# One values' scale per pair of heads, q and k casts on ScalarE, and a planner that prices float32r weight loads

## The chip, the cores and the metric

One core of a Trainium2 chip runs the whole kernel. The metric is device time in microseconds (us) of one execution; lower is better. The engines are named as the profile names them: PE (TensorE matmuls), PEld (its weight loads), DVE (VectorE), ACT (ScalarE), POOL (GpSimd) and SP (SyncE, which issues every DMA of this kernel).

## What is computed

```python
# q, k, v: (2, 8, 768, 64); centroids: (8, 16, 64)
q_assign = argmax(einsum('bhsd,hcd->bhsc', unit(q), unit(centroids)), -1)
k_assign = argmax(einsum('bhsd,hcd->bhsc', unit(k), unit(centroids)), -1)
scores = where(q_assign[..., :, None] == k_assign[..., None, :], q @ k.T / 8, -1e9)
attn = softmax(scores)
x = heads_side_by_side(attn @ v)                 # (1536, 512)
h = x @ w_in;  x = (h - tanh(h)) @ w_out         # d_ff 2048
out = (sigmoid(x @ w_gate) * (x @ w_val)) @ w_out2   # d_ff 1536
```

## The kernel before

The 16 heads (2 batches of 8) go through attention in 8 pairs; then two feed-forward blocks run over 1536 tokens. Each float32 operand is split into a high float32r part and a low rest, and a product is three matmuls, or one with the parts stacked on the partitions. Exponentials and values are split in the same way into two float16 parts; for that the values are first multiplied by a power of two, the *scale* `sv`.

A head passes these steps. `pair_prep(s)`: SP loads `rawq` and `rawk` of the pair, PE transposes them (line 504), ACT copies them out into `xtq`, `xtk` (L508), PE makes the cluster scores (L532), DVE finds the largest in five operations (L544 to L554), PE transposes the one-hot rows (L566), ACT writes them to `oht` (L572). The high parts of q and k, `hlq` and `hlk`, are cast by DVE (L513), the low parts by POOL (L520). SP then copies q, k and one-hot rows into a stack of each head (`stk`, three buffers; L245). `head_max(h)`: six tiles of 128 queries; PE computes each tile's high-part scores into one of three PSUM buffers (`ba`, `bb`, `bc`; L638), DVE takes each row's maximum (L642); PE and DVE turn the maxima into one row (`mt`), and SP puts it into the stack. `head_attend(h)`: six tiles again; PE makes the full scores (L673, L674), ACT takes each tile's exponential twice, in float32 (`pf`) and in float16 (`pt` or `ptt`; L677), POOL or DVE subtracts the two (L687), and PE multiplies with the values (L704 to L706, 108 matmuls a head), after which DVE divides (L719 to L721).

The scale: `v_scale(b)` makes one number for each batch. Four loads by `v_part` bring the whole batch's values into `pt` buffers, which are not otherwise used yet; DVE takes the largest magnitude of each (L441) and of the four (L458), PE transposes the result (L459), DVE makes a power of two and its reciprocal in four one-partition operations (L453 to L456), PE spreads it to all partitions (L461), DVE writes `sv` (L463). Each pair's values are loaded a second time into the one buffer `rawv` (L612), scaled by ACT to the high part (L616) and by DVE to the low part (L619).

Nothing of this order is written by hand. Every step is a `Task` with an engine, a cost, a priority, the tasks it needs and the buffers it takes. `Planner.run` walks through time as it models it and gives each engine, again and again, the ready task with the least priority number among those that can start within `AH_<engine>` of the first one. The instructions are issued in that order, and each engine, SP's queue too, keeps it on the chip. The table `PRM` holds the numbers from which priorities are made (`ZH` for the casts, `ZOT` for the one-hot rows, and so on). While PE has nothing to do at the start, it runs `N_BUSY` = 140 fillers of two matmuls (L423).

In the planner of before a PE task costs a fixed time, doubled while the planner thinks that the clock is low:

```python
cost = t.cost if self.warm else 2 * t.cost
```

Of the kernel before, what the change touches and what calls it, by code (L numbers as in the profile page):

```python
# [18 lines left out]
P = 128  # L19
# [7 lines left out]
PRM = dict(  # L27
    QUEUE=2.4775, AH_PE=0.086, AH_ACT=0.2978, AH_DVE=0.0374, AH_POOL=1.0538, AH_SP=0.8944, N_BUSY=140, NR=2,
    NRH=1, HX=['hx', 'hhxx'], WAR=0.797, LM=9, LV=8, ZP1=-12.75, ZP=1.801, FD=0.173, FO=0.6467, LOQ=0, VHI=0,
    VL=2.416, VLS=1.907, VR=17.393, ZSV=-28.212, ZRAW=19.311, ZT=0.914, ZH=36.739, ZHL=14.119, ZS=4.321,  # L30
    ZC=-8.823, ZOT=-37.186, ZD=22.995, ZDH=0.679, ZDM=3.94, ZVL=25.343, ZVS=33.74, ZX=-1.228, ZE=36.766,
    ZLOW=18.842, ZLOWP=2.75, SEMS=1.0, TC=0.2839, TW=0.9257, M2=1, ZQK=0.25, ZMS=-24.119, Z0=52.817, HB=92.235,
    NB4=5, ROWS=0.0155, VB=7.706, RAWL=2.2, NMID=2, NPL2=2, W1L=0.695, D1L=0.565, W2L=1.385, D2L=-1.014,
    ZI=7.332, ZJ=-3.277, PORT=0.12)


class Task:
# [3 lines left out]
    __slots__ = ("eng", "cost", "lat", "fn", "deps", "prio", "take", "end", "n", "duty", "port")  # L41

    def __init__(self, eng, cost, prio, fn, deps=(), take=(), lat=0.0, duty=1.0, port=None):
        self.eng, self.cost, self.prio, self.fn = eng, cost, prio, fn
        self.port = eng == "POOL" if port is None else port
        self.deps, self.take, self.lat, self.duty = [d for d in deps if d is not None], list(take), lat, duty
        self.end = None
# [9 lines left out]
class Planner:  # L57
# [10 lines left out]
    def __init__(self):  # L68
        self.tasks, self.kinds, self.clock = [], {}, {}
        self.count, self.coming, self.retire = {}, {}, {}  # L70
        self.first = {}
        self.link, self.port = 0.0, 0.0
        self.busy, self.window, self.warm = {}, 0, False

    WINDOW = 3.413

    def tensor_time(self, start, t):
# [5 lines left out]
        cost = t.cost if self.warm else 2 * t.cost  # L83
        a, end = start, start + cost
        while a < end:
            w = int(a / self.WINDOW + 1e-9)
            e = min(end, (w + 1) * self.WINDOW)
            self.busy[w] = self.busy.get(w, 0.0) + (e - a) * t.duty
            a = max(e, a + 1e-6)
# [34 lines left out]
    def run(self):  # L124
# [16 lines left out]
        while todo:  # L141
            best = None
            for eng, lst in ready.items():
                now = self.clock.get(eng, 0.0)
                can = []
                for at, t in lst:
                    start = max(now, at)
                    if t.lat:
                        start = max(start, self.link - self.QUEUE)
                    for kind in {s.kind for s in t.take}:  # L150
                        n = sum(s.kind == kind for s in t.take)
                        free = sorted(f[0] + self.lag(f[1], eng) for f in self.kinds.get(kind, ()))
                        if len(free) < n:
                            break
                        start = max(start, free[n - 1])
                    else:
                        can.append((start, t.prio, t.n, t))
                if can:
                    first = min(c[0] for c in can)
                    c = min((c for c in can if c[0] <= first + self.AHEAD[eng]), key=lambda c: c[1:3])  # L160
# [49 lines left out]
def tile_cluster_attention_moe(  # L210
# [164 lines left out]
    sv = const.tile([P, B], F32, name="sv")  # L375
    vm = const.tile([P, B, HP + 1], F32, name="vm")
    e = const.tile([1, B, 2], F32, name="e")
# [33 lines left out]
    t_c3 = add(PE, 0.11, -30, lambda: nc.tensor.transpose(at(z_sm)[0:D, 0:H * C], cn, ident), [t_c2], [z_sm])  # L411
# [13 lines left out]
    fill = [add(PE, 0.107, 1e6, keep_busy) for i in range(N_BUSY)]  # L425
# [5 lines left out]
    t_sv = []  # L431

    def v_part(b, i, z):
        buf = Slot("pt")

        def flat_buf():
            return at(buf).bitcast(F32).rearrange("p a n -> p (a n)")
# [6 lines left out]
    def v_scale(b):  # L444
        z = PRM["VL"] + b * PRM["VB"]
        parts = [v_part(b, i, z + i * PRM["VLS"]) for i in range(HP)]
        z += HP * PRM["VLS"] + PRM["ZSV"]
        sc = Slot("sm")
        i32 = mybir.dt.int32
        x, y, top = e[:, b, 0:1], e[:, b, 1:2], vm[:, b, HP:]  # L450

        def v_top():
# [27 lines left out]
    def pair_prep(s):  # L480
# [8 lines left out]
        for x, (nm, src) in enumerate((("q", q), ("k", k))):  # L489
# [8 lines left out]
            ev[nm], tts = [], []  # L498
            for half in range(2):
# [10 lines left out]
                tt = use(raw, add(PE, 0.33, z + PRM["ZT"] + PRM["ZQK"] * x + half, tr, [ld] + tts, [sm] + ([xt] if half == 0 else [])))  # L510
                tts.append(tt)
                ev[nm].append(use(sm, add(ACT, c_act(HALF), z + PRM["ZT"] + PRM["ZQK"] * x + half, evac, [tt] + ev[nm])))
            hi_t[nm] = add(DVE, c_dve2(S), z + PRM["ZH"] + PRM["ZQK"] * x, lambda xt=xt, hls=hls: nc.vector.tensor_copy(  # L513
                at(hls)[:, 0], at(xt)), ev[nm], [hls], port=True)
            lo_t[nm] = []
            for half in range(2):
# [4 lines left out]
                                                            op=ALU.subtract), [hi_t[nm]]))  # L521
            use(xt, hi_t[nm], *lo_t[nm])
# [12 lines left out]
        s0 = add(PE, 0.86, z + PRM["ZS"] + 0.0, lambda: score(0), ev["q"] + ev["k"] + [t_cb], [sm], duty=0.75)  # L535
        s1 = add(PE, 0.86, z + PRM["ZS"] + 0.1, lambda: score(1), [s0], duty=0.75)
        s2 = add(PE, 0.86, z + PRM["ZS"] + 0.2, lambda: score(2), [s1], duty=0.75)
# [3 lines left out]
        def scores():  # L541
            return at(sm)[:, 0:G * C].rearrange("p (g c) -> p g c", c=C)

        m0 = add(DVE, c_dve(G * C), z + PRM["ZC"] + 0, lambda: nc.vector.tensor_reduce(  # L544
            at(mm)[:, 0, :, 0], scores(), axis=AX.X, op=ALU.max), [s2], [mm])
        m1 = add(DVE, c_dve(G * C), z + PRM["ZC"] + 0, lambda: nc.vector.tensor_tensor(
            scores(), scores(), at(mm)[:, 0].to_broadcast([P, G, C]), op=ALU.is_equal), [m0])
        m2 = add(DVE, c_dve(G * C), z + PRM["ZC"] + 0, lambda: nc.vector.tensor_tensor(
# [941 lines left out]
```

## Time and profile before

| | us |
|---|---|
| median of 3 runs (795.37 to 795.73) | 795.71 |
| the profiled execution's own time | 795.33 |
| its span, first to last instruction | 793.5 |
| busy in the span: PE / PEld | 777.7 / 728.7 |
| busy in the span: DVE / ACT / POOL | 576.0 / 438.0 / 565.0 |

Of the execution's time 1.8 us lie outside the span. Attention fills roughly the first 260 us and the feed-forward blocks the rest. Matmuls overlap in PE's pipeline, so that "busy" on PE says that something is in flight, not that PE is at its peak; two things have to be read beside it, the distance from one matmul's start to the next, and how many of the matmuls are fillers. The granted clock is TensorE's, as a share of 2.4 GHz.

### The profile page before, as it was taken

What the parts mean: (1) busy time and instruction counts of PE and PEld (TensorE: products, weight loads), DVE (VectorE), ACT (ScalarE), POOL (GpSimd) and SP (SyncE); (2) the same over time, 40 slices, a digit from 0 to 9 for tenths busy, and PEclk for the clock granted to TensorE, in tenths of its full rate; (3) what the DMA queues carried; (4) which work ended last, traced back from release to release, by engine and by line L of the source; (5) the groups of instructions that cost most, each with busy time, mean ns of one, the idle gap of its engine ahead of it and who ended that gap; (6) DMA issues with size and microseconds to landing.
All of it is one profiled execution on the core that took longest, in us unless ns stands there. A gap on an engine that the chain in (4) does not pass through costs nothing.

```text
span 793.5 us, 15831 instructions
## 1 busy us (share of the span) xinstructions
PE 777.7 (98%) x5919; PEld 728.7 (92%) x5919; DVE 576.0 (73%) x1076; ACT 438.0 (55%) x852; POOL 565.0 (71%) x597
## 2 busy tenths in 40 slices
PE   9999999999999999999999999999999999999998
PEld 9777889888879999999999999999999989999996
DVE  4967987797987878967577678996456576666424
ACT  4267787878886645544454455655553535344240
POOL 4078777876898995888678688979584856748331
PEclk9989999999999999999999999999999999999999
DMA  9775666465543000422122132113211222221004
GB/s 220 201 173 139 155 156 138 110 152 141 150 135 102 29 1 0 134 67 80 57 78 67 42 113 86 40 56 106 67 40 67 81 80 81 67 66 41 1 1 159
DMA packets 69340, 72.93 MB, mean 92 GB/s; under 512 B 30256, under 2 KB 52880, under 8 KB 69264
## 3 DMA queue, kind: packets, MB, share of 16 engines
q1 hardware_dynamic: 69264, 71.93, 33.0%
q8 instruction: 46, 0.75, 0.4%
q14 instruction: 30, 0.25, 0.1%
HBM read 48.27 MB, written 3.15 MB: 65 GB/s over the span
## 4 chain that ended last, share of the span: by engine, by line
PE 84%; DVE 8%; issue 5%; ACT 2%; POOL 1%; DMA 0%; DVEq 0%; POOLq 0%; ACTq 0%
PE over_left L974 18%; PE over_left L1293 16%; PE over_right L974 13%; PE over_right L1293 9%; PE sm L974 6%; PE sm L1293 6%; DVE finr L642 2%; PE sm L704 2%; PE sm L705 2%; PE sm L706 1%; PE sm L532 1%; PE sm L504 1%; PE bb L673 1%; PE ba L673 1%; PE ba L638 1%
## 5 line engine op out<-in xcount | busy, mean ns | idle before, releaser
L687 POOL TENSOR_TENSOR pt<-pf,pt 128x768 f16<-128x768 f32 x45 | 75.5, 1691 | 28.1 <-ACT pt L677 13.1
L687 POOL TENSOR_TENSOR ptt<-pf,ptt 128x768 f16<-128x768 f32 x34 | 58.0, 1724 | 41.2 <-ACT ptt L677 34.1
L1000 ACT ACTIVATE stk<-pf 128x384 fp32r<-128x384 f32 x43 | 22.6, 524 | 37.7 <-POOL pf L1323 12.4
L1001 POOL TENSOR_TENSOR stk<-pf,hlq 128x384 fp32r<-128x384 f32 x22 | 22.7, 1030 | 27.8 <-ACT hlq L1000 27.8
L1293 PE MATMUL over_left<-xh,stk 128*128 128x384 f32 x138 | 41.5, 336 | 0.0
L974 PE MATMUL over_left<-stk,w 128*128 128x384 f32 x158 | 39.4, 335 | 0.0
L704 PE MATMUL sm<-vs,pt 128*128 128x65 f16 x324 | 38.2, 194 | 0.4 <-DVE xl L741 0.4
L642 DVE TENSOR_REDUCE finr<-ba 128x1 fp32r<-128x768 f32 x35 | 33.2, 947 | 7.1 <-PE ba L638 7.0
L705 PE MATMUL sm<-vs,pt 128*128 128x64 f16 x324 | 38.1, 195 | 0.0
L706 PE MATMUL sm<-vs,pt 128*128 128x65 f16 x324 | 37.7, 192 | 0.2 <-POOL pt L687 0.2
L1313 DVE TENSOR_TENSOR pf<-over_left,pf 128x384 f32<-128x384 f32 x42 | 23.3, 554 | 19.8 <-ACT pf L1309 12.3
L642 DVE TENSOR_REDUCE finr<-bc 128x1 fp32r<-128x768 f32 x32 | 30.3, 948 | 6.6 <-PE bc L638 6.4
L704 PEld LDWEIGHTS <-pt 128*128 128x128 f16 x324 | 29.9, 96 | 5.5 <-issue 5.4
L677 ACT ACTIVATE pf<-bb 128x768 f32<-128x768 f32 x34 | 27.9, 822 | 10.8 <-PE bb L674 7.4
L677 ACT ACTIVATE pf<-ba 128x768 f32<-128x768 f32 x31 | 25.5, 823 | 15.0 <-PE ba L674 13.2
L1001 POOL TENSOR_TENSOR stk<-pf,stk 128x384 fp32r<-128x384 f32 x25 | 26.6, 1063 | 7.7 <-ACT stk L1000 7.5
L705 PEld LDWEIGHTS <-pt 128*128 128x128 f16 x324 | 30.3, 97 | 0.7 <-issue 0.5
L706 PEld LDWEIGHTS <-pt 128*128 128x128 f16 x324 | 30.4, 99 | 0.3 <-POOL pt L687 0.3
L642 DVE TENSOR_REDUCE finr<-bb 128x1 fp32r<-128x768 f32 x29 | 27.5, 947 | 4.3 <-PE bb L638 4.2
L705 PE MATMUL sm<-vs,ptt 128*128 128x64 f16 x252 | 30.2, 195 | 0.3 <-DVE vs L619 0.3
L704 PE MATMUL sm<-vs,ptt 128*128 128x65 f16 x252 | 30.3, 193 | 0.0
L706 PE MATMUL sm<-vs,ptt 128*128 128x65 f16 x252 | 30.1, 192 | 0.0
(575 smaller groups left out, 3167.8 us busy)
## 6 DMA issues: line engine op xcount, KB each, us to landing
vs<-in_moe_w_out_dram SPq DMA_DIRECT2D x48, 256.0 KB, 2.6
stk<-hlq SPq DMA_DIRECT2D x32, 192.0 KB, 2.7
stk<-hlk SPq DMA_DIRECT2D x16, 384.0 KB, 4.2
vs<-in_moe_w_in_dram SPq DMA_DIRECT2D x24, 256.0 KB
vs<-in_moe_w_gate_dram SPq DMA_DIRECT2D x24, 256.0 KB
vs<-in_moe_w_val_dram SPq DMA_DIRECT2D x24, 256.0 KB, 2.7
rawq<-in_q_dram SPq DMA_DIRECT2D x16, 192.0 KB, 3.0
rawk<-in_k_dram SPq DMA_DIRECT2D x16, 192.0 KB, 4.6
```

The source lines that it names most:

```text
L642: rd.append(use(mx, add(DVE, c_dve(S), z + t, lambda t=t, mx=mx: nc.vector.tensor_reduce(at(mh)[:, t:t + 1], at(mx)[:, :, 0:HALF], axis=AX ...
L673: nc.tensor.matmul(o, at(sk)[0:K1, 1, ts], at(sk)[0:K1, 0, c], start=True, stop=False)
L677: nc.scalar.activation(o.rearrange("p (j n) -> p j n", j=2), at(st)[:, :, 0:HALF], AF.Exp, scale=scale)
L687: lambda nce=nc.vector if on_v else nc.gpsimd, pf=pf, pt=pt: nce.tensor_tensor(at(pt)[:, 1], at(pf), at(pt)[:, 0], op=ALU.subtract), [e0, ...
L704: nc.tensor.matmul(oview()[:, t], ph, vv[:, 0:D + 1], start=(kt == 0), stop=False)
L705: nc.tensor.matmul(oview()[:, t, 0:D], ph, vv[:, D + 1:2 * D + 1], start=False, stop=False)
L706: nc.tensor.matmul(oview()[:, t], plo, vv[:, 0:D + 1], start=False, stop=(kt == T - 1))
L974: nc.tensor.matmul(ps, a, b, start=(i == 0), stop=(i == n - 1))
L1000: a = add(ACT, c_acts(CH), z, lambda: nc.scalar.activation(hi(), src(), AF.Copy), deps, take)
L1001: b = add(POOL, c_pool(CH), z, lambda: nc.gpsimd.tensor_tensor(lo(), src(), hi(), op=ALU.subtract), [a])
L1293: nc.tensor.matmul(at(bank[to])[:, 0:CH], lh, rh, start=start and i == 0, stop=stop and i == 3 * KH - 1, skip_group_check=True)
L1313: return use(x, use(bank[n], add(DVE, c_dve(CH), rank[0], lambda: nc.vector.tensor_tensor(at(x), ps(n), at(x), op=ALU.add), deps)))
```

## The change

- **Scale.** `v_scale` is called from `pair_prep` and makes one scale for each pair of heads out of the pair's own `rawv`, which is there for the scaling anyway. The eight extra loads into `pt` and the reduction over four parts are gone; the chain of DVE reduction (now L447), PE transpose (L451), four DVE operations (L442 to L445), PE spread (L453) and `sv` (L455) runs 8 times where it ran twice. The scaling on ACT and DVE now waits for its own pair's chain.
- **Casts.** With `NHA` = 8 all 16 casts of q and k to the high part go from DVE (`nc.vector.tensor_copy`) to ACT (`nc.scalar.activation`, L503).
- **Planner.** A PE task carries the time `tail` of its last matmul. A task of float32r matmuls (no `tail` given) costs up to `LOAD` = 0.111 more when PE comes to it with no matmul before it that is long enough to load its weights behind. `duty` is gone.
- **Numbers.** `N_BUSY` is 155 and nearly all of `PRM` is new. `PVG` = 1 leaves the tasks of the value products as they were.

```diff
-    ZC=-8.823, ZOT=-37.186, ZD=22.995, ZDH=0.679, ZDM=3.94, ZVL=25.343, ZVS=33.74, ZX=-1.228, ZE=36.766,
+    ZOT=-40.532, ZD=21.696, ZDH=1.444, ZDM=3.94, ZVL=25.343, ZVS=16.581, ZX=-1.228, ZE=23.426, ZLOW=24.325,
...
         cost = t.cost if self.warm else 2 * t.cost
+        if t.tail is None:
+            cost += max(0.0, self.LOAD - (self.tail if start - self.clock.get("PE", 0.0) < 0.02 else 0.0))
+        self.tail = self.LOAD if t.tail is None else t.tail
...
-        ld = add(SP, DMA_C, z, lambda: dma(flat_buf().rearrange("p (h n) -> p h n", h=2), v[
-            b, 2 * i:2 * i + 2].rearrange("h (p t) d -> p h (t d)", t=T)), take=[buf], lat=1.2)
-        return use(buf, add(DVE, c_dve(2 * T * D), z + PRM["VR"], lambda: nc.vector.tensor_reduce(
-            vm[:, b, i:i + 1], flat_buf(), axis=AX.X, op=ALU.max, apply_absolute_value=True), [ld]))
...
-        t1 = add(DVE, 0.08, z, lambda: nc.vector.tensor_reduce(top, vm[:, b, 0:HP], axis=AX.X, op=ALU.max), parts)
-        t2 = add(PE, 0.11, z, lambda: nc.tensor.transpose(at(sc)[0:1, 0:P], top, ident), [t1], [sc])
+        t1 = add(DVE, c_dve(2 * T * D), z + PRM["VR"], lambda: nc.vector.tensor_reduce(
+            top, at(rv).rearrange("p h t d -> p (h t d)"), axis=AX.X, op=ALU.max, apply_absolute_value=True), [ld])
+        use(rv, t1)
+        z += PRM["ZSV"]
+        t2 = add(PE, 0.11, z, lambda: nc.tensor.transpose(at(sc)[0:1, 0:P], top, ident), [t1], [sc], tail=0.111)
...
-            hi_t[nm] = add(DVE, c_dve2(S), z + PRM["ZH"] + PRM["ZQK"] * x, lambda xt=xt, hls=hls: nc.vector.tensor_copy(
-                at(hls)[:, 0], at(xt)), ev[nm], [hls], port=True)
+            if s < PRM["NHA"]:
+                hi_t[nm] = [add(ACT, c_acts(S), z + PRM["ZH"] + PRM["ZQK"] * x, lambda xt=xt, hls=hls: nc.scalar.activation(
+                    at(hls)[:, 0], at(xt), AF.Copy), ev[nm], [hls])]
...
+        t_sv = v_scale(s, rv, lv, z + (PRM["ZV0"] if s == 0 else 0), smk)
...
-                    [lv, t_sv[b]] + [x[0] for x in vts], [vs] if hh == 0 else [])
+                    [t_sv] + [x[0] for x in vts], [vs] if hh == 0 else [])
```

Where the instructions stand now is shown at three places.

SP's queue around the first copy of a maxima row (`stk_0<-mt_0`, head 0). Before:

```order
L439 DMA pt_5_101<-in_v_dram 128x2x384
L245 DMA stk_0_86<-mt_0_115 1x6x128
L439 DMA pt_6_102<-in_v_dram 128x2x384
L439 DMA pt_7_103<-in_v_dram 128x2x384
L494 DMA rawq_0_120<-in_q_dram 128x6x64 x2
L494 DMA rawk_0_123<-in_k_dram 128x6x64 x2
L245 DMA stk_1_87<-mt_1_116 1x6x128
L245 DMA stk_2_88<-hlq_0_122 64x768
L612 DMA rawv_0_92<-in_v_dram 128x2x384
L245 DMA stk_0_86<-hlq_0_122 64x768
L245 DMA stk_2_88<-hlk_0_125 64x2x768
```

With the change:

```order
L483 DMA rawk_0_123<-in_k_dram 128x6x64 x2
L249 DMA stk_0_86<-mt_0_115 1x6x128
L249 DMA stk_2_88<-hlq_0_122 64x768
L606 DMA rawv_0_92<-in_v_dram 128x2x384
L249 DMA stk_2_88<-hlk_0_125 64x2x768
L249 DMA stk_2_88<-oht_0_128 16x768 x2
L249 DMA stk_2_88<-hlq_0_122 32x768
L249 DMA stk_2_88<-hlk_0_125 32x768
```

The loads of values into `pt` are gone from here, and the copies into `stk_2`, the stack of head 2, stand right behind the first `mt`; before they stood behind the second one and behind four loads.

ACT in the exponentials of head 1. Before (`pf` and `pt` are exponentials, `vs` values, `oht` one-hot rows):

```order
L677 ACTIVATE pf_0_107<-bc_0_618 128x768
L616 ACTIVATE vs_1_90<-rawv_0_92,sv_170 128x6x64
L677 ACTIVATE pf_2_109<-bb_0_80 128x768
L616 ACTIVATE vs_1_90<-rawv_0_92,sv_170 128x6x64
L677 ACTIVATE pf_1_108<-ba_0_76 128x768
L677 ACTIVATE pt_2_98<-ba_0_76 128x768
L677 ACTIVATE pf_0_107<-ba_0_76 128x768
L572 ACTIVATE oht_0_128<-sm_1_72,row_b_163,row_w_160 64x768
```

With the change (`hlk` is a cast):

```order
L672 ACTIVATE pf_2_109<-bc_0_637 128x768
L672 ACTIVATE ptt_8_104<-bc_0_637 128x768
L672 ACTIVATE pf_0_107<-ba_0_76 128x768
L672 ACTIVATE ptt_8_104<-ba_0_76 128x768
L672 ACTIVATE pf_1_108<-bc_0_637 128x768
L672 ACTIVATE ptt_10_105<-bc_0_637 128x768
L503 ACTIVATE hlk_0_125<-xtk_0_124 128x768
L566 ACTIVATE oht_0_128<-sm_1_72,row_b_163,row_w_160 64x768
L672 ACTIVATE pf_2_109<-bb_0_80 128x768
L672 ACTIVATE ptt_10_105<-bb_0_80 128x768
```

The scaling of values has left this stretch, and a cast stands in it.

The scale of the fourth pair, on PE from the transpose of the maxima to the spread, and on DVE. With the change:

```order
L451 MATMUL sm_1_72<-ident_136,vm_171 1x128
L668 MATMUL bb_0_80<-stk_2_88 128x384
L669 MATMUL bb_0_80<-stk_2_88 128x384
L668 MATMUL bb_0_80<-stk_2_88 128x384
L669 MATMUL bb_0_80<-stk_2_88 128x384
L633 MATMUL ba_0_76<-stk_0_86 128x384 x2
L453 MATMUL sm_1_72<-e_172,ones1_166 128x2
```

```order
L447 TENSOR_REDUCE vm_171<-rawv_0_92 128x1
L637 TENSOR_REDUCE finr_1_114<-ba_0_76 128x1
L442 TENSOR_REDUCE e_172<-sm_1_72 1x1
L443 TENSOR_SCALAR e_172<-e_172 1x1
L444 TENSOR_SCALAR e_172<-e_172 1x1
L445 RECIPROCAL e_172<-e_172 1x1
L637 TENSOR_REDUCE finr_1_114<-ba_0_76 128x1
L455 TENSOR_SCALAR sv_170<-sm_1_72 128x1
```

Before, nothing of this stood here: both scales were made earlier. On PE six matmuls lie between the two small ones; on DVE a reduction of a head's maxima stands between the values' reduction and the four operations.

## Rows read from the trace of the kernel before

**Rows 1.** Stretches: length, busy us of PE, PEld, DVE, ACT, POOL, granted clock, DMA.
```profile
0.00:36.00 36.00, 33.35 (x393) 30.57 (x393) 22.57 (x40) 10.85 (x19) 8.19 (x38) 1.00 0.84 204
36.00:66.00 30.00, 27.20 (x223) 21.90 (x223) 23.99 (x38) 21.16 (x33) 19.62 (x13) 0.89 0.75 180
66.00:80.00 14.00, 13.19 (x155) 11.53 (x156) 9.89 (x17) 10.69 (x18) 13.11 (x10) 0.88 0.58 131
80.00:260.00 180.00, 174.58 (x2269) 156.38 (x2268) 152.38 (x253) 144.88 (x226) 143.25 (x103) 1.00 0.55 136
260.00:785.00 525.00, 524.70 (x2861) 504.78 (x2862) 364.40 (x728) 250.41 (x560) 380.83 (x437) 1.00 0.19 62
```

**Rows 2.** Timeline of the DMA queue SP: start us, issuing time, copies issued.
```profile
12.80 1.13 SPq L439 DMA_DIRECT2D pt<-in_v_dram  x2
...
17.08 1.23 SPq L245 DMA_DIRECT2D stk<-oht  x2
...
32.74 0.84 SPq L245 DMA_DIRECT2D stk<-mt  x1
...
39.96 0.55 SPq L245 DMA_DIRECT2D stk<-hlq  x1
```

**Rows 3.** Issues by line: size of each and median us to landing.
```profile
stk<-hlq SPq DMA_DIRECT2D x32, 96.0 KB, 2.3
```

**Rows 4.** Timeline of PE, 20 to 53 us.
```profile
21.48 2.17 PE L423 MATMUL sm<-busy 128*128 128x128 bf16 x36
24.20 0.59 PE L638 MATMUL ba<-stk 80*128 80x384 f32 x2 [0.55 <-DMA stk<-oht]
...
34.57 0.38 PE L461 MATMUL sm<-e,ones 1*128 1x2 f32 x2
...
36.15 0.45 PE L673 MATMUL bc<-stk 112*128 112x384 f32 x1 [0.31 <-DVE finr L642]
...
51.26 0.38 PE L461 MATMUL sm<-e,ones 1*128 1x2 f32 x2
51.57 0.62 PE L638 MATMUL ba<-stk 80*128 80x384 f32 x2
```

**Rows 5.** Timeline of DVE, 27 to 35 us.
```profile
31.39 0.96 DVE L642 TENSOR_REDUCE finr<-ba 128x1 fp32r<-128x768 f32 x1
32.44 0.28 DVE L648 CAST mt<-sm 6x128 fp32r<-6x128 f32 x1
...
33.51 0.27 DVE L453 TENSOR_REDUCE e<-sm 1x1 f32<-1x128 f32 x1
```

**Rows 6.** Timeline of ACT, 37 to 66 us.
```profile
37.17 0.81 ACT L677 ACTIVATE pf<-bc 128x768 f32<-128x768 f32 x1 [0.77 <-PE bc L674]
37.88 0.80 ACT L677 ACTIVATE ptt<-bc 128x768 f16<-128x768 f32 x1
...
47.92 0.90 ACT L508 ACTIVATE xtk<-sm 128x384 f32<-128x384 f32 x2
...
58.30 0.81 ACT L677 ACTIVATE pf<-ba 128x768 f32<-128x768 f32 x1 [5.70 <-PE ba L674]
...
65.28 0.81 ACT L677 ACTIVATE pt<-ba 128x768 f16<-128x768 f32 x1
```

**Rows 7.** Timeline of PE, 66 to 73 us.
```profile
67.44 0.52 PE L674 MATMUL bb<-stk 97*128 97x384 f32 x1
...
72.40 0.19 PE L706 MATMUL sm<-vs,pt 128*128 128x65 f16 x1
72.43 0.42 PE L673 MATMUL bc<-stk 112*128 112x384 f32 x1
72.69 0.34 PE L674 MATMUL bc<-stk 97*128 97x384 f32 x1
72.87 0.34 PE L673 MATMUL bc<-stk 112*128 112x384 f32 x1
```

**Rows 8.** Groups of DVE in 80 to 260 us: busy, mean ns; idle before.
```profile
L513 DVE CAST hlk<-xtk 128x768 fp32r<-128x768 f32 x5 | 5.8, 1156 | 0.0
```

More of the change, by code (lines that the diff above doesn't have):

```diff
@@ L87, in tensor_time @@
             e = min(end, (w + 1) * self.WINDOW)
-            self.busy[w] = self.busy.get(w, 0.0) + (e - a) * t.duty
+            self.busy[w] = self.busy.get(w, 0.0) + e - a
             a = max(e, a + 1e-6)
@@ L146, in run @@
                 for at, t in lst:
[L147 to L153, printed above, removed]
+                    start = max(now, at, self.link - self.QUEUE) if t.lat else max(now, at)
+                    for kind, n in t.needs:
+                        if (kind, eng) not in free:
+                            free[kind, eng] = sorted(f[0] + self.lag(f[1], eng) for f in self.kinds.get(kind, ()))
+                        if len(free[kind, eng]) < n:
                             break
-                        start = max(start, free[n - 1])
+                        start = max(start, free[kind, eng][n - 1])
                     else:
@@ L158, in run @@
                 if can:
-                    first = min(c[0] for c in can)
-                    c = min((c for c in can if c[0] <= first + self.AHEAD[eng]), key=lambda c: c[1:3])
+                    end = min(can, key=lambda c: c[0])[0] + self.AHEAD[eng]
+                    c = min((c for c in can if c[0] <= end), key=lambda c: c[1:3])
                     if best is None or c[0] < best[0]:
@@ L538, in pair_prep @@
+        s1 = add(PE, 0.86, z + PRM["ZS"] + 0.1, lambda: score(1), [s0], tail=0.111)
+        s2 = add(PE, 0.86, z + PRM["ZS"] + 0.2, lambda: score(2), [s1], tail=0.111)
         use(xts["q"], s0, s1, s2)
         use(xts["k"], s0, s1, s2)
[L541 to L545, printed above, removed]
@@ L553, in onehot, with groups, of_g @@
-        def onehot():
-            nc.vector.tensor_tensor(at(oh).rearrange("p t x h c -> p (t x h) c"), scores(),
-                                    at(mm)[:, 1].to_broadcast([P, G, C]), op=ALU.is_equal)
-        m4 = add(DVE, c_dve(G * C), z + PRM["ZC"] + 1, onehot, [m3], [oh])
+        def groups(t):
+            return at(t)[:, 0:G * C].rearrange("p (g c) -> p g c", c=C)
+        def of_g(i):
+            return at(mm)[:, i].to_broadcast([P, G, C])
+        ohv = lambda: at(oh).rearrange("p t x h c -> p (t x h) c")
@@ new lines, in pair_prep @@
+        z_m = z + PRM["ZC"]
+        m0 = add(DVE, c_dve(G * C), z_m, lambda: nc.vector.tensor_reduce(
+            at(mm)[:, 0, :, 0], groups(sm), axis=AX.X, op=ALU.max), [s2], [mm])
+        m1 = add(DVE, c_dve(G * C), z_m, lambda: nc.vector.tensor_tensor(
+            groups(sm), groups(sm), of_g(0), op=ALU.is_equal), [m0])
+        m2 = add(DVE, c_dve(G * C), z_m, lambda: nc.vector.tensor_tensor(
+            groups(sm), groups(sm), first.unsqueeze(1).to_broadcast([P, G, C]), op=ALU.mult), [m1])
@@ L558, in pair_prep @@
+        m3 = add(DVE, c_dve(G * C), z_m + 1, lambda: nc.vector.tensor_reduce(
+            at(mm)[:, 1, :, 0], groups(sm), axis=AX.X, op=ALU.max), [m2])
+        m4 = add(DVE, c_dve(G * C), z_m + 1, lambda: nc.vector.tensor_tensor(
+            ohv(), groups(sm), of_g(1), op=ALU.is_equal), [m3], [oh])
         use(sm, m4)
@@ L697, in head_attend, with pv @@
         pvs = []
-        for t in range(T):
-            def pv(t=t):
-                ts = slice(t * P, (t + 1) * P)
-                for kt in range(T):
+        NV = PRM["PVG"]
+        for t0 in range(0, T, NV):
+            def pv(t0=t0):
+                for t, kt in ((t, kt) for t in range(t0, t0 + NV) for kt in range(T)):
+                    ts = slice(t * P, (t + 1) * P)
                     ph, plo = at(pts[kt])[:, 0, ts], at(pts[kt])[:, 1, ts]
```

100 lines of the change are left out of this document (44 added, 56 removed).

## The prediction

> **What bounds the kernel now.** I read the stretches of the run first, because the bound changes between them [rows 1]. From 260 to 785 us PE is busy 524.7 of 525 us: the feed-forward blocks run at PE's pace, and no other engine is above 381. The change touches no instruction there, so this stretch can only move as a whole. From 80 to 260 us PE is idle for 180 - 174.6 = 5.4 us; DVE is busy for 152.4, ACT for 144.9, POOL for 143.3. PE bounds here too, but three engines stand close behind it. Up to 36 us PE looks just as busy (33.4), but much of that is filler work, as the 36 fillers right before the first maxima at 24.20 us show [rows 4]; here the DMA share is 0.84 and the work is a chain of latencies. From 36 to 66 us nothing is full: ACT is busy for 21.2 of 30 us, DVE for 24.0.
>
> Second, SP and PE in the ramp. The first maxima wait for a one-hot copy: SP issues it from 17.08 to 18.31 us, and the matmul starts at 24.20, released by it [rows 2, 4]. So it took 5.9 us to land, where such copies of 96 KB land in 2.3 at the median [rows 3]. What stood before it in the queues were loads of values into `pt`, two of them issued at 12.80 [rows 2]. The first exponentials can come only after the first full scores, at 36.15 [rows 4].
>
> Third, ACT from there on. One exponential starts 0.71 us after the other (37.17, 37.88), so 24 of them, heads 0 and 1, need 17.0 us; the last one ends at 65.28 + 0.81 = 66.1, 28.9 us after the first began [rows 6]. The largest hole is 5.70 us before 58.30, released by PE: PE was making head 2's maxima, which began only at 51.57 [rows 4], since SP copied that head's q only at 39.96, behind the second maxima row [rows 2]. This hole is the thing that the new order can close.
>
> **The change part by part.** All sums are against the profiled execution, 795.33 us; it lies 0.4 under the median of 795.71, and I carry the difference over to the median.
>
> *Ramp to the first full scores.* Before the first one-hot copy four loads of 393 KB into `pt` were issued; in the change none, and the load of the third pair's q (393 KB) moves there. That is 1.18 MB less, 5.8 us at the 204 GB/s of the stretch [rows 1]. The copy can gain at most what it lost, 5.9 - 2.3 = 3.6 us. Some of it is given back on DVE: before head 0's maxima row is cast (32.44 before [rows 5]), DVE now also runs the second pair's value reduction, taken as the 0.96 of a reduction of the same size, the four one-partition operations, under the 1.06 from 33.51 to the spread at 34.57 [rows 4, 5], and a subtraction of half that size, about 0.5. I take 0.96 + 0.8 + 0.5 = 2.3 back: **-1.3 us**, between -3.6 and +0.5.
>
> *Exponentials of heads 0 and 1.* With the change the copies for head 2 stand right behind the first maxima row, which the queue issued at 32.74 [rows 2]; they can go some 6 us earlier, and head 2's maxima fill PE while ACT works on heads 0 and 1. What ACT does in the stretch: 21.16 us of work [rows 1], less one copy-out (0.45, from 0.90 for two), plus one cast, taken as 0.71, the step of an exponential of the same 768 elements [rows 6]: 21.4. If ACT never waited, the 28.9 us would become 21.4; if nothing closed, they stay. I leave it 2 us of waits, about a quarter of its 8.8 idle us before, because it still shares three PSUM buffers with the maxima: 23.4, so **-5.5 us**, between -7.5 and 0. By that point PE has done the same work in both orders but for 36 of 108 value matmuls and six one-hot transposes, which come later now: 36 x 0.03 (72.40 to 72.43 [rows 7]) and 6 x 0.06 (a filler, 2.17 / 36 [rows 4]) are **+1.4 us**. The 30 further fillers lie where PE waits for DMA, DVE or ACT; without that cover they cost 30 x 0.06 = 1.8.
>
> *Clock.* In 36 to 66 and in 66 to 80 us the granted clock is 0.89 and 0.88 [rows 1]: PE ran at 1.2 instead of 2.4 GHz for about 6.6 and 3.4 us; a matmul then takes 0.52 us instead of 0.34 [rows 7]. The first is inside the term above. Of the second, 1.7 us lost, I take half back: **-0.8 us**, between 0 and -1.7.
>
> *Order of PE.* A float32r matmul after another kind starts its successor 0.26 us later instead of 0.18 (72.43, 72.69, 72.87 [rows 7]). Counted in the two orders, fillers left out, there are 103 such places before and 113 with the change: the planner now prices them, yet its new numbers make more of them. 10 x 0.08 is **+0.8 us**.
>
> *Scale on PE.* Five of the eight scales now fall where PE bounds, none did. A spread takes 0.31 (51.26 to 51.57 [rows 4]); for the transpose I take 0.1, between nothing and the same 0.31: 5 x 0.41 = 2.1. PE must also wait if DVE's four operations are not done when it comes to the spread. They need 1.06; in front of it lie, by the order, six to 40 matmuls, worth 1.1 to 2.3 us. The fourth pair has the least, six of 0.18, and DVE may be in a reduction of 0.96 first. I take 0.7 for all five: together **+2.8 us**, between +0.5 and +9.
>
> *DVE and ACT later on.* DVE loses the casts; those of k cost 1.16 us each on average between 80 and 260 [rows 8], as POOL runs beside them. It gains a reduction of 0.96 and about 0.9 of small work a pair, so in sum it is not worse off. ACT gains 11 casts x 0.71 = 7.8 on 144.9 of 180 us, and stays at 85%. So no engine takes over by its sum, and I let the 5.4 us in which PE idles shrink by half, since reductions of maxima no longer queue behind casts: **-2.7 us**, between -5.4 and +8. Here two pages of the Trainium skill speak against the change. "VectorE: DVE Perf Modes" (the perf-mode tier table) says that a float32 copy from SBUF to SBUF runs at two elements a cycle on VectorE, and "ScalarE: Activation LUTs" (What ACT_TABLE_LOAD costs) that ScalarE does one; worked out from their figures that is an estimate of 0.46 us on DVE against 0.83 on ACT, and the 11 casts would be 9.1 us of ACT instead of 7.8: this term would stay, and the slower rival below would be 802.2. The trace differs from the first page, with 1.16 on DVE here [rows 8], and gives 0.71 a step on ACT [rows 6].
>
> *Sum:* -1.3 - 5.5 + 1.4 - 0.8 + 0.8 + 2.8 - 2.7 = -5.3 us. That is 790.0 for the profiled execution and **790.4** for the median. A measurement of this kernel can tell about 0.2%, 1.6 us, from no change: faster is under 794.1, slower over 797.3.
>
> **The rivals.** *More than that.* ACT closes all its waits in the ramp (-2.0 more), PE's idle time goes altogether (-2.7), the clock does not fall (-0.9), no spread waits (-0.7): 784.1. For it speaks that sums of all engines leave room; against it that all of them would have to fit.
>
> *Nothing comes of the ramp.* If DVE's maxima bound it, not the copies and not ACT, the first two terms and their +1.4 go: -5.3 + 6.8 - 1.4, 795.8, no change. DVE's 24.0 of 30 us [rows 1] speak for it; the hole of 5.70 that PE released, not DVE, speaks against it. Nearly the same time comes when each of the five spreads finds two reductions of 0.96 ahead of DVE's operations: 1.06 + 1.92, less 1.6 of matmuls, 1.4 each, 7.0 instead of the 0.7: 796.7.
>
> *Casts in the way, slower.* ACT keeps its order. A cast that stands between a tile's scores and its exponentials holds a PSUM buffer and so PE. If each of the 11 later casts shows in full, and PE's idle time does not shrink, 7.8 + 2.7 come on top: 800.9. It is slower than before from 0.38 us a cast on. For it: ACT's largest hole was released by PE [rows 6], so that the two run tile by tile. Against it: ACT has 35 us of slack in 180, and casts can sit in it.
>
> **How the numbers follow.** I give 0.60 to the forecast, 0.17 to the larger gain, 0.10 to the two ways to no change, and 0.13 to slower. Faster is then 0.77, same 0.10, slower 0.13. The range of 783.5 to 797.5 takes in the bounds up to the larger gain and no change, and leaves out the slower case.
>
> **What would show it.** Right: the first full scores at about 35 us; the last exponential of head 1 at about 59.5 instead of 66.1; no hole over 2 us in ACT there; head 2's maxima well before 51 us; PE idle by under 4 us in the 180 us that follow the ramp; the feed-forward stretch as long as before, only earlier. Wrong: PE waiting at the spread for the reciprocal on DVE by over 1 us a pair; exponentials released by ACT's own cast; a clock under 1.0 beyond the ramp; a gain in the feed-forward blocks, for which I see no reason.

## The result, and the profile after

The changed kernel takes 788.27 us (median of 7 runs, 785.29 to 790.92), the kernel before 795.71 beside it. The ratio is 0.9913 with a 95% interval of [0.9885, 0.994]: 6.9 us faster, and the interval does not reach 1. The forecast was 790.4 in a range of 783.5 to 797.5. The profiled execution took 787.04 us, span 785.0, against 795.33 and 793.5. Single runs of one kernel differ by several us: the seven of before beside it lie between 791.80 and 796.35, and of the changed kernel one has a span of 783.2 at a granted clock of 1.000, another 788.9 at 0.997. Measured again later, the two kernels took 787.57 and 793.76, 6.2 us apart.

The stretches of the changed kernel, as in [rows 1] (length; busy us of PE, PEld, DVE, ACT, POOL; granted clock; DMA share; GB/s):

```profile
0.00:36.00 36.00, 35.01 (x415) 32.73 (x415) 22.53 (x45) 15.71 (x26) 12.42 (x42) 1.00 0.73 171
36.00:66.00 30.00, 29.62 (x322) 26.22 (x321) 24.92 (x42) 27.90 (x43) 22.11 (x16) 1.00 0.67 154
66.00:80.00 14.00, 13.59 (x164) 12.95 (x162) 10.99 (x18) 11.99 (x20) 9.74 (x7) 1.00 0.74 162
80.00:260.00 180.00, 174.79 (x2238) 159.30 (x2237) 147.65 (x267) 148.60 (x236) 147.19 (x111) 0.99 0.52 130
260.00:785.00 525.00, 521.02 (x2836) 500.28 (x2834) 359.47 (x718) 244.16 (x548) 369.65 (x425) 1.00 0.20 63
```

From 36 to 66 us ACT rose from 21.2 to 27.9 us and PE has 322 matmul records where it had 223. Neither this stretch nor the next shows a lowered clock, where [rows 1] had 0.89 and 0.88. From 80 to 260 us PE is idle for 5.2 us, before 5.4: nothing gained there.

The queue SP of the changed kernel, as in [rows 2]:

```profile
17.84 1.25 SPq L249 DMA_DIRECT2D stk<-oht  x2
...
32.27 0.86 SPq L249 DMA_DIRECT2D stk<-mt  x1
33.24 0.56 SPq L249 DMA_DIRECT2D stk<-hlq  x1
```

Its PE, as in [rows 4]:

```profile
22.65 0.60 PE L633 MATMUL ba<-stk 80*128 80x384 f32 x2
...
35.24 0.42 PE L668 MATMUL ba<-stk 112*128 112x384 f32 x1
...
41.17 0.38 PE L453 MATMUL sm<-e,ones 1*128 1x2 f32 x2
41.48 0.62 PE L633 MATMUL bb<-stk 80*128 80x384 f32 x2
```

Its ACT, as in [rows 6]:

```profile
36.23 0.81 ACT L672 ACTIVATE pf<-ba 128x768 f32<-128x768 f32 x1 [0.15 <-PE ba L669]
...
48.20 0.81 ACT L672 ACTIVATE pf<-bb 128x768 f32<-128x768 f32 x1 [1.32 <-PE bb L669]
...
58.26 0.79 ACT L672 ACTIVATE ptt<-bb 128x768 f16<-128x768 f32 x1
```

The first maxima start at 22.65 instead of 24.20 us, the first full scores at 35.24 instead of 36.15, head 2's maxima at 41.48 instead of 51.57. ACT's hole of 5.70 us is gone; the longest left is 1.32. The last exponential of head 1 ends at 58.26 + 0.79 = 59.05 us instead of 66.1, so the 24 exponentials took 22.8 us from the first start instead of 28.9.

For what follows I use one count over a whole trace, **lost time** on PE: the steps between the starts of consecutive matmuls, less what the same shape takes back to back at full clock (0.174 us for 384 columns of float32r, 0.029 for a value matmul, 0.11 for a transpose of float32), fillers counted as lost. Total span is useful work plus lost time. It gives each run a number for the ramp (the stretch up to 80 us) and one for the stretch behind it. Two things limit it. It is of the one profiled execution, and that need not be the median one: without the later chains it was the slowest of six (788.73), with the extra loads the fastest of twelve (787.35). And the marks at 80 and 260 us are fixed in time, so that a late run carries waits over them; where two runs have the same order I also compare the start of each matmul with its own in the other run, and call that *matmul by matmul*.

| run | median us, ratio to before [95%] | lost by 80 us | lost 80 to 260 |
|---|---|---|---|
| before | 795.71 (later 793.8 to 794.1) | 36.5 | 23.6 |
| changed | 788.27, 0.9913 [0.9885, 0.994] | 27.4 | 22.5 |
| changed, again | 787.57, 0.9922 [0.9891, 0.9953] | 26.8 | 22.4 |
| changed, no later chains | 785.92, 0.9904 [0.9882, 0.9927] | 27.7 | 25.5 |
| changed, casts on DVE, same order | 793.26, 0.9993 [0.9977, 1.0008] | 28.9 | 26.5 |
| changed, later casts on DVE, same order | 792.47, 0.9982 [0.9963, 1.0001] | 29.8 | 26.5 |
| changed, extra loads | 792.06, 0.9974 [0.9952, 0.9996] | 28.6 | 21.0 |
| before, no V loads | 793.43, 0.9992 [0.9977, 1.0008] | 34.4 | 23.2 |
| before, one chain | 794.08, 1.0008 [0.9989, 1.0027] | 35.8 | 23.3 |
| before, casts on ACT | 799.34, 1.0061 [1.0041, 1.0082] | 36.6 | 24.8 |
| changed, casts on DVE, order anew | 806.84, 1.0171 [1.0136, 1.0205] | 34.1 | 34.1 |
| changed, loads unpriced, order anew | 809.15, 1.0188 [1.0153, 1.0223] | 29.2 | 36.0 |
| before with the new numbers, order anew | 810.0, 1.0192 [1.0153, 1.0231] | 33.5 | 36.7 |
| changed with the old numbers, order anew | 798.26, 1.0045 [1.0025, 1.0066] | 30.8 | 30.3 |

Between the two kernels 9.1 us of lost time went before 80 us and 1.1 from there to 260; behind that it is 5.5 and 5.4. The span fell by 8.5, so about 1.8 us of useful work was added: the six further scale chains, two of them before 80 us (0.6) and four behind it (1.2). On the work that both kernels share, the changed one is thus 8.5 us ahead at 80 us and gains nothing more after it.

### The profile page after: what moved, and what is told of

Its sections match the earlier page's. It is cut to its first block, busy times and chain, and to the rows that moved or that the text cites. A ratio compares the mean times of both kernels' runs of the same rounds, so it can differ in the third digit from the quotient of the medians.

```text
span 785.0 us, 15929 instructions
## 1 busy us (share of the span) xinstructions
PE 774.0 (99%) x5967; PEld 731.5 (93%) x5967; DVE 565.6 (72%) x1088; ACT 448.4 (57%) x868; POOL 561.1 (71%) x597
## 4 chain that ended last, share of the span: by engine, by line
PE 90%; DVE 5%; ACT 2%; issue 1%; DMA 1%; SPq 0%; POOL 0%; DVEq 0%; ACTq 0%; POOLq 0%
PE over_left L970 18%; PE over_left L1289 16%; PE over_right L970 14%; PE over_right L1289 8%; PE sm L970 6%; PE sm L1289 5%; PE sm L427 3%; PE sm L700 2%; DVE finr L637 2%; PE sm L701 2%; PE sm L702 2%; PE sm L525 1%; PE ba L633 1%; PE bb L668 1%; PE bc L633 1%; PE bb L633 1%
## 5 line engine op out<-in xcount | busy, mean ns | idle before, releaser
L997 POOL TENSOR_TENSOR stk<-pf,hlq 128x384 fp32r<-128x384 f32 x20 | 20.7, 1035 | 34.2 <-ACT hlq L996 34.1
L1289 PE MATMUL over_left<-xh,stk 128*128 128x384 f32 x152 | 45.1, 336 | 0.0
L1309 DVE TENSOR_TENSOR pf<-over_left,pf 128x384 f32<-128x384 f32 x38 | 21.1, 555 | 25.8 <-ACT pf L1305 17.4
L997 POOL TENSOR_TENSOR hlq<-pf,hlk 128x384 fp32r<-128x384 f32 x27 | 27.7, 1027 | 13.8 <-ACT hlk L996 13.8
L700 PEld LDWEIGHTS <-pt 128*128 128x128 f16 x330 | 30.7, 97 | 5.2 <-issue 4.6
L970 PE MATMUL over_left<-stk,w 128*128 128x384 f32 x142 | 34.8, 335 | 0.0
L996 ACT ACTIVATE stk<-pf 128x384 fp32r<-128x384 f32 x38 | 19.9, 524 | 25.9 <-POOL pf L1319 6.9
L1305 ACT ACTIVATE pf<-over_left 128x384 f32<-128x384 f32 x39 | 19.0, 486 | 25.5 <-PE over_left L1289 24.8
L513 POOL TENSOR_TENSOR hlk<-xtk,hlk 128x384 fp32r<-128x384 f32 x16 | 16.6, 1054 | 22.9 <-ACT hlk L503 20.9
L701 PEld LDWEIGHTS <-pt 128*128 128x128 f16 x330 | 31.0, 97 | 1.2 <-issue 1.0
L672 ACT ACTIVATE pf<-bc 128x768 f32<-128x768 f32 x34 | 28.2, 830 | 6.4 <-PE bc L669 3.8
L702 PEld LDWEIGHTS <-pt 128*128 128x128 f16 x330 | 31.1, 99 | 0.0
L944 POOL TENSOR_TENSOR w<-ry,w 128x256 fp32r<-128x256 f32 x29 | 22.2, 775 | 12.1 <-ACT w L942 10.7
```

Source lines behind the costliest of these rows:

```text
L672: nc.scalar.activation(o.rearrange("p (j n) -> p j n", j=2), at(st)[:, :, 0:HALF], AF.Exp, scale=scale)
L700: nc.tensor.matmul(oview()[:, t], ph, vv[:, 0:D + 1], start=(kt == 0), stop=False)
L701: nc.tensor.matmul(oview()[:, t, 0:D], ph, vv[:, D + 1:2 * D + 1], start=False, stop=False)
L702: nc.tensor.matmul(oview()[:, t], plo, vv[:, 0:D + 1], start=False, stop=(kt == T - 1))
L944: e1 = add(POOL, c_pool(PIECE), z, lambda o=o, cut=cut: nc.gpsimd.tensor_tensor(at(w[1])[:, o], f32_of(cut), at(w[0])[:, o], op=ALU.subtra ...
L970: nc.tensor.matmul(ps, a, b, start=(i == 0), stop=(i == n - 1))
```

## The experiments

My theory after the result: the loads of V (the values) that are gone let the ramp run early, and the casts and the planner's price count little. Seven runs keep a kernel's order and exchange only instructions, so that one part moves alone; four let the planner make the order anew; one repeats the changed kernel.

**The extra scale chains.** In the changed kernel, for pairs 3 to 7:

```diff
+    LAST = 3
...
+        on = s < LAST
-        t1 = add(DVE, ..., lambda: nc.vector.tensor_reduce(
+        t1 = add(DVE, ..., lambda: on and nc.vector.tensor_reduce(
...
-                at(vs)[:, hh, :, 0:D], at(rv)[:, hh], AF.Copy, scale=sv[:, s:s + 1]),
+                at(vs)[:, hh, :, 0:D], at(rv)[:, hh], AF.Copy, scale=sv[:, s % LAST:s % LAST + 1]),
```

> The changed kernel in its own order, with the scale chains of the five later pairs (3 to 7) left out: their reduction, transposition, v_top, spread and last multiplication are not issued, and these pairs use the scale of pair s mod 3 (so five of the eight scales are not computed). The prediction priced these chains at +2.8 us on the path (2.1 us of matmuls and turned weight loads on TensorE, 0.7 us of waits of the spreads). If that price is right, the time falls to about 785.5 us (from 788.3). The rival: the chains fall into gaps that TensorE has anyway, then 787.5 to 788.5 us. The trace of the changed kernel shows the spreads' waits at 0.4 + 0.5 us in all, so I lean to something between, 786.5 us.

785.92 us. The changed kernel measured again with later runs:

> The changed kernel as it is, beside the runs that follow, so that they are compared on one chip. Nothing is left out. 787 to 788.5 us; 6 to 7 us under the kernel before. If the extra chains of the five later pairs cost what the prediction said, this is 2 to 3 us above the 785.9 us of the run without them; if they cost nothing, within 1 us of it.

787.57 us. The five chains are worth 1.7 us by the medians, but the two intervals overlap widely, so that nothing and 3 us are both possible. Matmul by matmul the traces say what a chain costs in its place: with its spread and its transpose left out, PE comes through 0.5 us sooner at three of the five, 0.1 at one, and no sooner at the fourth pair's, 1.6 us in all. (The profiled run lost 2.5 us elsewhere, at 215 to 227 us, where it waited for a stack copy and its clock fell; that is why the table shows 25.5.) The trace of the changed kernel shows that the waits I feared are absent: PE's weight loads for the spreads between 80 and 260 us, 8 for four chains, stood idle for 0.4 us in all.

```profile
L453 PEld LDWEIGHTS sm<-e,ones 1*128 1x128 f32 x8 | 1.2, 183 | 0.4 <-issue 0.2
```

**The traffic.** In the kernel before, the eight loads for the scale and their reductions are dropped:

```diff
+    nc.gpsimd.memset(vm, 0.5)
-        ld = add(SP, DMA_C, z, lambda: dma(flat_buf()...
+        ld = add(SP, DMA_C, z, lambda: None and dma(flat_buf()...
-        return use(buf, add(DVE, ..., lambda: nc.vector.tensor_reduce(
+        return use(buf, add(DVE, ..., lambda: None and nc.vector.tensor_reduce(
```

> The kernel before in its own order, with the eight V loads for the scale and their eight reductions left out (the maxima are a constant, so the scale is not computed from V; the rest of the chain runs). My theory (the loads' 3.1 MB on the link early, and the waits behind them, make the ramp late): the largest hole of ScalarE in 36 to 66 us goes from 5.7 us to under 2 us, TensorE keeps its full clock there, and the time is 788 to 791 us. The rival (the gain of the change comes from the new order and the casts, the traffic was hidden): 794 to 796 us, with the hole before the stack copies of head 2 still there.

793.43 us, ratio 0.9992, between the two ranges and nearer to the rival's: my theory fell. The first maxima came at 22.89 us, 1.3 earlier, and head 1's last exponential ended at 62.73, 3.4 earlier; but the hole stayed, and so did the lowered clock (0.94 from 36 to 66 us, 0.88 from 66 to 80). Matmul by matmul the run is 3.6 us ahead of before at 51 us and 2.1 at 76; of the medians 0.7 us is left, which the interval does not tell from nothing. ACT of this run:

```profile
54.63 0.81 ACT L678 ACTIVATE pf<-ba 128x768 f32<-128x768 f32 x1 [4.44 <-PE ba L675]
```

Its DVE stood still just before:

```profile
45.66 0.28 DVE L454 TENSOR_REDUCE e<-sm 1x1 f32<-1x128 f32 x1 [4.36 <-PE sm L460]
...
48.11 0.16 DVE L464 TENSOR_SCALAR sv<-sm 128x1 f32<-128x1 f32 x1 [1.63 <-PE sm L462]
48.73 0.96 DVE L643 TENSOR_REDUCE finr<-ba 128x1 fp32r<-128x768 f32 x1 [0.46 <-PE ba L639]
```

The other way round, the changed kernel gets four loads of 393 KB more, two behind the load of pair 0's values and two behind the first stack copy of head 1 (the expectation says pair 1; the edit has `hd == 1`, which is a head):

```diff
+    def more_v(n):
+        for i in (n, n + 1):
+            dma(tiles["pt", 4 + i]..., v[0, 2 * i:2 * i + 2]...)
```

> The changed kernel in its own order, with four extra loads of V of 393 KB each into buffers that are not in use yet, two behind the load of pair 0's values and two behind the first stack copy of pair 1 (nobody reads them). By the traffic theory each holds the link for some 2.3 us at the 171 GB/s of the ramp: head 1's last exponential ends 3 to 6 us later than 59.05 us and the time is 791 to 794 us. If the traffic is hidden and only the order counts: 788 to 789 us.

792.06 us, ratio 0.9974 [0.9952, 0.9996]. In its profiled run they cost 1.2 to 1.8 us before 80 us and then nothing more: span 785.3 at a clock of 1.000. Head 1's last exponential ended at 60.98 us, 1.9 later, where I had expected 3 to 6: the time fell into the expected range, but not in the way that I gave for it. Its other runs have spans of 787.1 to 796.1 at clocks of 0.993 to 0.999, and no trace tells where they lost it. So more traffic made the kernel slower, by a way that is not shown, but the absence of the old traffic does not make the gain.

**A chain in DVE's queue.** New theory: DVE waits in its queue for the second batch's chain, and head 2's maxima wait behind. In the kernel before, `b == 0 and` stands ahead of every operation of that chain, and `sv[:, 0:1]` is used for both batches.

> The kernel before in its own order, without the second batch's part of the scale: its four loads, four reductions, transposition, v_top, spread and last multiplication are not issued, and the second batch uses the first one's scale (so one of the two scales is not computed). In the run without the eight loads VectorE still stood 4.36 us and 1.63 us in its queue between 41.2 and 48.7 us, behind the second batch's chain, whose transposition and spread wait in TensorE's queue, and the hole before 58 us hardly shrank. Theory (that chain in VectorE's queue, not the traffic, makes the hole): the waits are gone, the largest hole of ScalarE between 45 and 62 us is under 4 us instead of 5.7, and the time falls by 2 to 4 us, to 790 to 792 us. Rival (TensorE's own order makes the hole: full scores of head 1, then the first scores of pair 1, then the maxima of head 2): the hole stays over 5 us and the time is 793 to 794 us.

794.08 us: this theory fell as well. The rival is nearer, in time above all; the hole, which it put at over 5 us, is 4.46. DVE of this run waits still longer, now for the maxima themselves, which PE begins at 51.30 us:

```profile
52.00 0.96 DVE L642 TENSOR_REDUCE finr<-ba 128x1 fp32r<-128x768 f32 x1 [6.83 <-ACT pf L677]
```

and ACT has the hole:

```profile
58.58 0.81 ACT L677 ACTIVATE pf<-ba 128x768 f32<-128x768 f32 x1 [4.46 <-PE ba L674]
```

Whatever is taken from the other queues, PE comes to head 2's maxima only after the full scores that ACT paces and the second pair's first scores. But PE's order is only the last part of it. Head 2's maxima also need the one-hot copies in its stack, and SP's order brings these late too. In the kernel before:

```profile
43.63 2.29 SPq L245 DMA_DIRECT2D stk<-oht  x2
```

By the profile the second of them landed at 47.9 us, without the V loads at 46.6, with one chain at 49.7; head 2's maxima began at 51.57, 48.00 and 51.30. In the changed kernel the two copies were issued from 35.18 us and the maxima began at 41.48. So in these three runs the copies alone kept the maxima until 5 to 8 us after that, and PE's order added 1.4 to 3.7. No run changed one of the two orders without the other. The clock was 1.00 in all five stretches of this run, so the half clock of [rows 1] was not what made the ramp long either.

**The engine of the casts.** In both kernels the engine is exchanged within the kernel's own order. Changed kernel:

```diff
-                ... lambda xt=xt, hls=hls: nc.scalar.activation(
-                    at(hls)[:, 0], at(xt), AF.Copy), ev[nm], [hls])]
+                ... lambda xt=xt, hls=hls: nc.vector.tensor_copy(
+                    at(hls)[:, 0], at(xt)), ev[nm], [hls])]
```

> The changed kernel in its own order, with the sixteen q and k casts issued on VectorE in place of ScalarE, at the place in VectorE's order where the order's program meets them. My theory (the gain is the ramp's, by the V loads that are gone from the link; the engine of the casts matters little): 788 to 790.5 us, and the last exponential of head 1 ends within 1 us of 59.05 us. The rival (the gain is VectorE's relief by the casts): most of it is lost, 793 to 796 us, with VectorE as what ends TensorE's waits between 80 and 260 us.

793.26 us: in time the rival's number. Head 1's last exponential ends 1.6 us later, which is only the smaller part of it. A second run keeps pairs 0 and 1 on ACT (`if s < 2`):

> The changed kernel in its own order, with the casts of the pairs 2 to 7 issued on VectorE and those of the pairs 0 and 1 left on ScalarE. With all sixteen on VectorE, it lost 5.7 us: by the profiles 1.6 us of it before 80 us and 4.0 us between 80 and 260 us. If the loss sits in the steady part, where VectorE's queue sets when scores come free, this run keeps most of it: 791 to 792.5 us. If it sits in the ramp: 788 to 789.5 us.

792.47 us, 4.9 above the changed kernel's 787.57, where all casts on DVE gave 5.7: most of the loss comes with the casts of pairs 2 to 7. Matmul by matmul, PE falls behind the changed kernel by 3.3 us up to 80 us and by 3.1 more up to 260 (with all casts on DVE by 2.0 and 3.5). One step before 80 us is the wait that the prediction named as a sign of being wrong, at the spread of the fourth pair's scale:

```profile
62.82 0.38 PE L453 MATMUL sm<-e,ones 1*128 1x2 f32 x2 [1.17 <-DVE e L445]
```

On DVE a cast now stands right in front of the four small operations that it waits for:

```profile
60.83 1.20 DVE L504 CAST hlq<-xtq 128x768 fp32r<-128x768 f32 x1
61.96 0.27 DVE L442 TENSOR_REDUCE e<-sm 1x1 f32<-1x128 f32 x1
```

In the changed kernel no cast stands there, the spread starts at 60.75 us and shows no wait; with all casts on DVE it waits 1.17 us as well. So it is the casts on ACT that keep this scale off PE's path. Behind this wait the clock was 0.79 from 64 to 72 us; with all casts on DVE the same wait left it at 1.00. The stretch from 80 us on of this run is

```profile
80.00:260.00 180.00, 172.03 (x2246) 155.68 (x2246) 155.17 (x279) 141.81 (x223) 146.45 (x106) 0.99 0.53 132
```

with DVE at 155.2 instead of 147.7 us, and PE waits longer for DVE (what PE waited for in that stretch: us in total, times, longest):

```profile
PE bc L633 <- DVE finr L637: 1.2, 1, 1.2
...
PE sm L641 <- DVE oh L550: 0.7, 1, 0.7
PE sm L560 <- DVE mt L643: 0.7, 1, 0.7
```

Of these waits the changed kernel has one, and shorter:

```profile
PE sm L641 <- DVE oh L550: 0.2, 1, 0.2
```

These are 2.6 us against 0.2, and at these three places PE falls behind by 2.7 of the 3.1 us. The 4.0 us in the table are more because the late run meets behind the mark of 80 us some of what the changed kernel meets before it. The reverse, the kernel before with its casts on ACT:

> The kernel before in its own order, with the sixteen casts of q and k issued on ScalarE in place of VectorE. In the changed kernel's order the opposite move cost 5.7 us. If ScalarE is simply the better engine for them: 788 to 791 us. If each order has the casts where its own slack is (my theory after the runs so far): no gain or a loss, 793.5 to 798 us, since in this order ScalarE has the one-hot rows and the exponentials queued where the casts come.

799.34 us, 0.6% slower. ACT is not the better engine as such; that in the old order the casts come while it is late already is my reading and was not tried. The hole stays, now ended by DVE, head 1's last exponential ends at 67.45 instead of 66.1 us, and matmul by matmul the profiled run (798.29) is 0.2 us behind at 76 us and 2.5 at 254.

```profile
58.92 0.81 ACT L677 ACTIVATE pf<-ba 128x768 f32<-128x768 f32 x1 [5.19 <-DVE finr L642]
```

**The order made anew.** `NHA=8` becomes `NHA=0`:

> The changed kernel with the casts of q and k back on VectorE (the switch for it set to 0 pairs), and the order made anew by the planner for that. The run that only moved the instructions within the fixed order took 793.3 us, nearly all of the gain. Theory one (the loss there is VectorE's time itself: sixteen casts and the waits they bring in the first 260 us): it stays, 792 to 795 us. Theory two (the loss is that the order was made for casts on ScalarE): the planner finds its way round it and this run takes 787.5 to 790 us.

806.84 us, worse than either theory said. `LOAD = 0.111` becomes `LOAD = 0.0`:

> The changed kernel with the planner's price for turned and float32r weight loads set to zero, all numbers else as they are, and the order made anew. If the price is part of the gain: 1.5 to 4 us slower than the changed kernel (789.5 to 792 us), with the float32r matmuls more often alone between float16 ones. If it is not: within 1 us of it (787 to 789 us). The prediction held that the number of such places rises by ten and that this costs 0.8 us; the trace of the changed kernel does not show that cost, so I lean to no difference from the price itself, but an order made for other prices can come out 2 us to either side.

809.15 us. Its stretch behind the ramp shows a clock of 0.94:

```profile
80.00:260.00 180.00, 170.07 (x2121) 151.82 (x2120) 137.37 (x238) 144.59 (x218) 134.51 (x91) 0.94 0.51 126
```

In the kernel before, every number that both have is taken from the changed one, and the reverse:

> The kernel before with the changed kernel's numbers wherever both have the number (those that place its own loads for the scale are kept), and the order made anew. If the new numbers alone were the gain: 787 to 791 us. If they suit only the work they were chosen for, as the two remade orders so far (806.8 and 809.2 us) suggest: slower than before, 798 to 815 us.

810.0 us.

> The changed kernel with the kernel before's numbers wherever both have the number, and the order made anew: pair scale, casts on ScalarE and priced weight loads are all there, the priorities are the old ones. If the parts carry the gain by themselves: 787 to 792 us. If the gain needs numbers found for them: 797 to 815 us.

798.26 us. Neither the numbers nor the parts carry the gain alone. The last two columns of the table tell why. By 80 us, the eight rows of the changed kernel other than "casts on DVE, order anew" (34.1) have lost 26.8 to 30.8 us, even with the old numbers or without the price, and the five rows of the kernel before 33.5 to 36.6, even with the new numbers: there the parts count, under any numbers tried, and the casts on ACT among them where the order is made anew (34.1 without them), though not in the kept order (28.9). From 80 to 260 us only the orders whose numbers were found for their work, and those that keep such an order, lose 21 to 26.5 us; the four made anew lose 30.3 to 36.7. These runs do not show what the price of a weight load is worth by itself: an order made for other prices differs in thousands of places, and only with numbers found for each could the two be compared. That was not tried.

## Why the prediction was right, and where it was not

*Ramp to the first full scores*, -1.3: measured -0.9. Both halves were too large: the first maxima gained 1.55 us, and 0.6 was given back instead of 2.3. The first half rested on a wrong row: a one-hot copy is not one of the 96 KB copies that land in 2.3 us. Its own row, of the kernel before, has twice the time:

```profile
stk<-oht SPq DMA_DIRECT2D x32, 48.0 KB, 4.8
```

From issue to the first maxima it took 7.1 us before (17.08 to 24.20) and 4.8 now (17.84 to 22.65), so it gained 2.3 us, and it was issued 0.8 later. DVE cast the maxima row at 31.98, even earlier than before, with the first scale done by then:

```profile
28.06 0.27 DVE L442 TENSOR_REDUCE e<-sm 1x1 f32<-1x128 f32 x1
...
31.98 0.27 DVE L643 CAST mt<-smr 6x128 fp32r<-6x128 f32 x1
```

*Exponentials of heads 0 and 1*, -5.5: measured -6.1. The mechanism was the right one: SP's copies for head 2 come early, and its maxima fill PE while ACT works. The three runs that kept the old order and took away loads, a chain or DVE's casts left a hole of 4.4 us or more, and the runs that kept the new order, with chains, traffic or casts changed, needed 22.8 to 23.2 us as it does. In all fourteen traces the time goes with the start of head 2's maxima: 22.0 to 24.1 us where they begin by 45.6 us, 26.0 to 30.4 where they begin at 48.0 or later. What stays open is how much of it is SP's order and how much PE's.

*Deferred value matmuls*, +1.4: **this step failed.** I held that at head 1's last exponential PE had done the same work but for 36 value matmuls and six transposes. By the count it had done 33.0 us of useful work at 66.1 us before, and 33.8 at 59.05 now, 0.3 of it a third scale chain. What was put off was more than made up by matmuls drawn ahead, which I had not counted. It is worth -0.5, 1.9 us away from the term, most of the 2.3 us by which the ramp was underrated (-6.2 predicted to 80 us; -8.5 measured, which is -9.1 of lost time and +0.6 for the two chains).

*Clock*, -0.8: no stretch before 80 us shows a lowered clock, and about 1.0 of the 8.5 us is left for it beside the three terms above. A sign of being wrong, a clock under 1.0 beyond the ramp, did come in the profiled run, at 107.9 to 111.3 us with 0.59; the repeated run has 1.00 from 80 to 260, and its lost time there is the same (22.4 and 22.5).

*Order of PE*, +0.8, *scale*, +2.8, *idle time*, -2.7: together +0.9. Measured behind 80 us: +1.2 of added work, -1.2 of lost time, nothing in all. That this comes near the sum is luck, since two of its parts were far off: the five later scales cost 1.6 us in their places (2.1 for the work and 0.7 for waits were forecast, and the waits were nothing), and PE's idle time shrank by 0.2 instead of 2.7, so that the sign "PE idle by under 4 us" did not come (5.2). The price of PE's order was not measured by itself.

*Casts.* ACT's casts take 0.83 to 0.90 us, and no wait of PE between 80 and 260 us is ended by one; the slower rival did not come about. With the 0.83 that I had estimated from the Trainium skill's "ScalarE: Activation LUTs" (What ACT_TABLE_LOAD costs) these casts agree. The 0.46 that I had estimated for DVE from the Trainium skill's "VectorE: DVE Perf Modes" (the perf-mode tier table) the runs do not bear out. On DVE the casts of q and k took 0.77 and 0.95 us on average behind 80 us (single ones 0.54 to 1.33), in the run that put back those of pairs 2 to 7:

```profile
L504 DVE CAST hlk<-xtk 128x768 fp32r<-128x768 f32 x5 | 4.7, 947 | 0.0
L504 DVE CAST hlq<-xtq 128x768 fp32r<-128x768 f32 x5 | 3.9, 773 | 0.0
```

The weight that I gave to DVE's relief was too small in one respect: it doesn't shrink PE's idle time against before, but without it the new order loses most of its gain, a fifth of that at the fourth pair's spread alone.

## What to carry to other kernels

In a kernel whose order a planner makes, the parts of a change can't be priced by switching one off and planning again: the three remade orders of the changed kernel were 11 to 22 us slower than it, whichever input was touched. Keep the order and exchange the instruction, and read the two effects apart: what a part costs in its place, and what the new order does. With the order kept, two traces can be laid side by side matmul by matmul, and the steps between them show each place where time is lost. Where an engine has a hole, ask first what the engine that releases it was made to do in front of it, and when its operands were sent; taking load off other queues moved the median by 0.1% here. And when work is put off past a mark, count all the work on both sides of the mark, not only what the diff moves.

## What the runs showed of the hardware that was not expected

With the same instructions in the same order, the changed kernel's span was 783.2 us at a granted clock of 1.000 and 788.9 at 0.997. The clock is not all of the difference: 0.003 of 785 us is 2.4 us, an estimate, and another run had 785.0 at 0.997. One of its two profiles has PE at half clock, 1.2 GHz, in most of this stretch (columns as above), around waits of 0.64 and 0.57 us at 107.26 and 108.45:

```profile
107.90:111.30 3.40, 2.85 (x43) 2.58 (x43) 3.40 (x6) 3.09 (x5) 3.40 (x3) 0.59 0.04 8
```

The other profile has the same two waits (0.65 and 0.57 us) at full clock, and so has the run with extra loads (0.63 and 0.58). So the same order, with the same waits, can fall or not. Matmul by matmul the other profile is 1.5 us faster through this stretch, and then waits 1.3 us more at later places, for a stack copy and for ACT: at 260 us hardly anything of the clock's cost is left. It is otherwise in two of the four orders made anew: they show 0.94 from 80 to 260 us, and 0.06 x 180 is up to 10.8 (an estimate) of the 13.5 and 14.2 us that they lost there beyond the changed kernel. The other two show 0.98.
